# First loads of a fused sequence-mixing and gated-MLP kernel: x's first block in two halves, weights ahead of x's last blocks, another order of turns and quarters

## The chip, the cores and the metric

The kernel runs on one core of a Trainium2 chip. The metric is the device time of one execution in microseconds (us). A core has five engines that run side by side and wait for each other by semaphores: PE (TensorE, matrix products), DVE (VectorE), ACT (ScalarE), POOL (GpSimd) and SP (SyncE, which here only issues DMA transfers). Weight loads of PE are listed apart as PEld. ACT issues a few DMA transfers too. All transfers, whichever engine issues them, run on the core's 16 DMA engines.

## The reference

```python
x  = A_q                                  # 2048 x 640, bfloat16
xn = _layernorm(x, axis=-1)               # mean and variance of each row
return x + _A_ref(xn, A_k, A_v, A_shift_k, A_ssm_k, A_ssm_D) + _B_ref(xn, B_w_gate, B_w_up, B_w_down)

def _A_ref(q, k, v, shift_k, ssm_k, ssm_D):
    # k is filtered with four taps along the sequence, kv = k_shift * v,
    # y = kv convolved along the sequence with ssm_k (by FFT of twice the length) + kv * ssm_D
    return q * y

def _B_ref(x, w_gate, w_up, w_down):      # 640 x 1728, 640 x 1728, 1728 x 640
    g = jnp.einsum("bsd,df->bsf", x, w_gate)
    u = jnp.einsum("bsd,df->bsf", x, w_up)
    h = _sigmoid(g) * u
    return jnp.einsum("bsf,fd->bsd", h, w_down)
```

## The kernel before

The 2048 rows are 16 blocks of 128 rows, taken in four groups of four. x is a tile of 128 partitions by 16 blocks by 640 columns of two bytes, so one block is 160 KB. For each group the kernel normalises four blocks (`ln_stats` L198, `ln_aggr` L202, `ln_var` L210 on DVE, `ln_pow` L214 on POOL, `ln_xn` L219 on DVE). It then turns each block: `xn_mm` (L234) makes five 128x128 transposes on PE into a PSUM tile `pt`, and `xn_ev` (L223) copies them on ACT to `xnT`. After that come the gated products: for each of 13 chunks `fc` of 128 columns, and one last half chunk, PE makes `pg` (w_gate) and `pu` (w_up) from five matmuls each over all 512 rows of the group (`product`, L257), ACT takes the sigmoid of `pg` (L266) and DVE multiplies it with `pu` into `hT` (L272). `down_mm` (L296) multiplies `hT` with w_down, and DVE adds the result to x (L301). The convolution (lines 309 to 466) has products of its own on PE, copies on ACT, multiplications on DVE and round trips of its intermediate results through HBM.

The program runs in the order in which it is written. After the prologue this order is the long string `ORDER` (L621), of which each letter is one step of one chain; each engine takes its own instructions strictly in that order, and the change does not touch the string.

The prologue, which the change does touch, is this:

- Loads. SP issues x's block 0 (L469), then 256 columns of w_gate, 320 KB (L173 by L473), then the next 256 columns of both weights (L475). ACT issues block 1 (L470), blocks 2 and 3 in one transfer of 320 KB (L471), and the first 256 columns of w_up, 320 KB (L176 by L473). Between its first and its second DMA, ACT has a table load and a warming activation (L119). A transfer of SP and one of ACT go through different queues, called q1 and q10 by the profile. The program has eight semaphores for its DMA transfers and uses them in turn, so a transfer can be issued only when the one eight before it has landed. The first that has to wait is SP's load of columns 512 to 768 of w_up, the second step of `ORDER`.
- `busy(15)` (L482): 15 matmuls of 128x512 on zeros, whose result is not used.
- Statistics and normalising of blocks 0 to 3, in this order on DVE: statistics of block 0; statistics of block 1, then xn of block 0; statistics of block 2, then xn of block 1; and so on. So xn of a block stands behind the statistics of the next block.
- `turn(0)`, that is `xn_mm` and `xn_ev` of block 0, and `busy(2)`.
- For the first two chunks of the first group the products are made in quarters (`quarter`, L248), five 128x128 matmuls for one block, one chunk and one of the two weights, so that PE can start with block 0 while the others are still on their way. There are 16 quarters. The turns of blocks 1 to 3 stand between them: turn 1 after two quarters of block 0, turn 2 after two quarters of block 1, and turn 3 after all four of block 1.
- Two sigmoids and two multiplications on the finished chunks; then the first dense product (L257) of `ORDER` begins.

PE takes its instructions in order: when a quarter waits for weights, the turn behind it waits too.

Of the kernel before, what the change touches and what calls it, by code (L numbers as in the profile page):

```python
# [57 lines left out]
def kernel(  # L58
# [14 lines left out]
    nc = tc.nc  # L73
    xr = A_q.flatten_outer_dims().rearrange("(p b) d -> p b d", b=NB)
# [30 lines left out]
    x = res.tile([P, NB, DM], BF16, name="x")  # L105
# [15 lines left out]
    sync = nc.sync  # L121
# [49 lines left out]
    def load_w(eng, lo, hi, u):  # L171
        if u == 0:
            eng.dma_start(w[:, :, lo:hi], wgr[:, :, lo:hi])  # L173
            return
        h = min(hi, 13 * P)
        eng.dma_start(w[:, :, UP + lo:UP + h], wur[:, :, lo:h])  # L176
        if hi == FF:
            eng.dma_start(w[:, :, FF:UP], wur[:, :, h:FF])
# [51 lines left out]
    def xn_mm(g, i):  # L230
        pool, tag = (psG, "g") if g else (psC, "c")
        xts[i] = pt = pool.tile([P, NC, P], BF16, name="pt", tag=tag)
        for c in range(NC):
            nc.tensor.transpose(pt[:, c, :], xn[:, 4 * g + i, c * P:(c + 1) * P], ident[:])  # L234

    def xn_ev(g, i, copy=act_copy):
        copy(out=xnT[:, i, :, :], in_=xts[i][:, :, :])
# [4 lines left out]
    def quarter(u, fc, i):  # L242

        if i == 0:
            pgs[u, fc] = psG.tile([P, 512], F32, name=("pg", "pu")[u], tag="g")
        o = u * UP + fc * P
        for c in range(NC):
            nc.tensor.matmul(pgs[u, fc][:, i * P:(i + 1) * P], lhsT=w[:, c, o:o + P], rhs=xnT[:, i, c, :],  # L248
                             start=(c == 0), stop=(c == NC - 1))
# [216 lines left out]
        nc.vector.tensor_tensor(xs, xs, chunks[c]["yx", m][:, :, :], ALU.add)  # L466


    sync.dma_start(x[:, 0, :], xr[:, 0, :])  # L469
    nc.scalar.dma_start(x[:, 1, :], xr[:, 1, :])  # L470
    nc.scalar.dma_start(x[:, 2:4, :], xr[:, 2:4, :])  # L471
    for u in range(2):
        load_w((sync, nc.scalar)[u], 0, 256, u)  # L473
    for u in range(2):
        load_w(sync, 256, 512, u)  # L475

# [3 lines left out]
    def busy(n):  # L480
        for _ in range(n):
            nc.tensor.matmul(idle[:, :], lhsT=hT[:, 0, 0:P], rhs=hT[:, 0, :], start=True, stop=True)  # L482

    def turn(i):
        xn_mm(0, i)
        xn_ev(0, i)


    busy(15)
    for i in range(4):  # L490
        ln_stats(0, i)
        if i:
# [5 lines left out]
    turn(0)  # L498
    busy(2)
    for i in range(4):  # L500
        for fc in range(2):
            for u in range(2):
                quarter(u, fc, i)
            if (i, fc) in ((0, 0), (1, 0), (1, 1)):
                turn(1 + i + fc)
    for fc in range(2):
        gate_ev(0, fc)
        up_ev(0, fc)
# [158 lines left out]
```

## Time and profile before

| what | value |
|---|---|
| median of 3 runs | 239.65 us (239.36 to 239.73) |
| the profiled execution | 239.41 us |
| its span, first to last instruction | 237.6 us |
| granted clock of PE | 1.00 in every stretch |
| PE, DVE, ACT busy | 231.4, 190.3, 141.2 us |
| first DMA packets, first statistics on DVE | after 1.5 us, at 3.97 us |
| first turn, first quarter, first dense product on PE | at 6.54, 7.78 and 14.34 us |

The span is the time between the first and the last instruction of the profiled execution; the rest of that execution's time lies around it. In the list of waits each row names who waited, for whom, the total in us, how often, and the longest. In the rows in order of time, the first number is the start from the beginning of the span, the second the duration, then engine, line, operation, result and operands, shape, how many instructions were merged, and in brackets the idle time before them with what ended it. Matmuls overlap in the pipeline, so of successive groups on PE the starts tell more than the durations. A row of the table by stretch gives the busy time of each engine in it, PE's granted clock, the share of time in which the DMA engines were busy, and the GB/s that they moved; these rates are added up to the bytes moved by a time:

| stretch, us | GB/s |
|---|---|
| 1.5 to 2.5 | 73 |
| 2.5 to 3.0 | 317 |
| 3.0 to 3.5 | 341 |
| 3.5 to 4.0 | 394 |
| 4.0 to 5.0 | 372 |
| 5.0 to 6.0 | 303 |
| 6.0 to 7.0 | 293 |
| 7.0 to 8.0 | 294 |

### The profile page before, as it was taken

The numbers are of one execution on the slowest core, as the hardware profiler recorded it, in microseconds if no ns is written. First come the engines' busy times: TensorE is split into PE (matmuls) and PEld (weight loads), VectorE is DVE, ScalarE is ACT, GpSimd is POOL, SyncE is SP. The second block draws the span as 40 slices with busy tenths as digits, with TensorE's granted clock in tenths as the row PEclk, the third lists the DMA queues.
The fourth block names the chain that finished last, engine by engine and source line by source line (L and its number), as shares of the span: only waits on it lengthen the run. The fifth ranks groups of instructions, "written<-read, shape, count | busy, mean of one in ns | idle before, by whom it ended". The sixth has DMA issues, their size and how long they took to land.

```text
span 237.6 us, 5553 instructions
## 1 busy us (share of the span) xinstructions
PE 231.4 (97%) x2265; PEld 135.1 (57%) x2265; DVE 190.3 (80%) x350; ACT 141.2 (59%) x178; POOL 11.2 (5%) x24
## 2 busy tenths in 40 slices
PE   8799999999999999999999999999999999999994
PEld 2564445878556455667754434577664434456782
DVE  3633889999999999999999999865585695968372
ACT  2342331728559897864888887997558858764000
POOL 4210000020000000002001000000000000000000
PEclk9999999999999999999999999999999999999999
DMA  7999999889998999999444888975939795285674
GB/s 212 292 314 233 259 322 298 183 249 284 253 311 243 253 295 297 284 267 319 148 183 152 234 230 258 227 228 203 241 109 222 186 281 123 89 238 144 196 237 134
DMA packets 88975, 54.82 MB, mean 231 GB/s; under 512 B 47670, under 2 KB 83062, under 8 KB 88694
## 3 DMA queue, kind: packets, MB, share of 16 engines
q1 hardware_dynamic: 88006, 53.66, 80.8%
q10 hardware_dynamic: 944, 0.82, 1.1%
q8 instruction: 17, 0.28, 0.5%
q14 instruction: 8, 0.07, 0.1%
HBM read 36.12 MB, written 18.35 MB: 229 GB/s over the span
## 4 chain that ended last, share of the span: by engine, by line
PE 95%; DMA 3%; ACT 0%; DVE 0%; ACTq 0%; issue 0%
PE pd L296 26%; PE pg L257 23%; PE pu L257 23%; PE psb L456 4%; PE ps L357 4%; PE ps L355 4%; PE ps L388 3%; DMA w<-in_B_w_up_dram 3%; PE psa L417 2%; PE pg L278 2%; PE pt L234 2%; PE pu L248 1%; PE pg L248 1%; ACT xnT L223 0%; DVE x L301 0%; ACT L119 0%
## 5 line engine op out<-in xcount | busy, mean ns | idle before, releaser
L257 PEld LDWEIGHTS <-w 128*128 128x128 bf16 x500 | 46.5, 98 | 54.3 <-issue 5.3
L296 PE MATMUL pd<-wd,hT 128*128 128x320 bf16 x448 | 64.3, 299 | 0.0
L257 PE MATMUL pg<-xnT,w 128*128 128x512 bf16 x250 | 62.2, 379 | 0.0
L257 PE MATMUL pu<-xnT,w 128*128 128x512 bf16 x250 | 62.1, 379 | 0.0
L296 PEld LDWEIGHTS <-hT 128*128 128x128 bf16 x448 | 42.8, 98 | 17.8 <-issue 1.7
L266 ACT ACTIVATE sig<-pg 128x512 bf16<-128x512 f32 x52 | 31.3, 605 | 30.1 <-PE pg L257 28.2
L272 DVE TENSOR_TENSOR hT<-sig,pu 128x512 bf16<-128x512 bf16 x52 | 35.2, 679 | 14.7 <-PE pu L257 9.3
L223 ACT CAST t<-ps 128x1024 bf16<-128x1024 f32 x40 | 39.1, 1023 | 11.4 <-DMA d<-t 6.3
L223 ACT CAST xz<-ps 128x1024 bf16<-128x1024 f32 x40 | 38.6, 1018 | 10.6 <-PE ps L388 10.5
L301 DVE TENSOR_TENSOR x<-pd,x 128x320 bf16<-128x320 f32 x32 | 15.4, 480 | 15.8 <-PE pd L296 15.7
L403 DVE TENSOR_TENSOR xz<-xz 128x2048 bf16<-128x2048 bf16 x20 | 24.4, 1220 | 0.2
L357 PE MATMUL ps<-kvh,S1t 128*128 128x128 bf16 x160 | 21.2, 219 | 0.0
L335 DVE TENSOR_TENSOR acc<-acc,tmp 128x1024 bf16<-128x1024 bf16 x30 | 20.7, 689 | 0.7
L355 PE MATMUL ps<-kvh,S1t 128*128 128x128 bf16 x160 | 21.2, 217 | 0.0
L333 DVE TENSOR_TENSOR tmp<-kx,sc 128x1024 bf16<-128x1024 bf16 x30 | 20.6, 687 | 0.4
L223 ACT CAST ao<-psa 128x1024 bf16<-128x1024 f32 x16 | 15.6, 1014 | 5.6 <-PE psa L417 3.5
L461 DVE TENSOR_TENSOR yx<-psb,xn 128x512 bf16<-128x512 f32 x20 | 13.8, 691 | 3.9 <-PE psb L456 2.9
L355 PEld LDWEIGHTS <-S1t 128*128 128x128 bf16 x160 | 15.5, 97 | 2.3
L357 PEld LDWEIGHTS <-S1t 128*128 128x128 bf16 x160 | 15.3, 96 | 2.3
L223 ACT COPY xnT<-pt 128x640 bf16<-128x640 bf16 x16 | 10.2, 709 | 10.8 <-PE pt L234 10.5
L198 DVE BATCH_NORM_STATS2 st<-x 128x6 f32<-128x320 bf16 x32 | 13.7, 471 | 2.8 <-DMA x<-in_A_q_dram 2.8
L401 DVE STREAM_SHUFFLE xz<-xz 128x512 f32<-128x512 f32 x20 | 14.6, 728 | 0.0
(44 smaller groups left out, 146.1 us busy)
## 6 DMA issues: line engine op xcount, KB each, us to landing
d<-t SPq DMA_DIRECT2D x20, 512.0 KB, 3.7
t<-d SPq DMA_DIRECT2D x20, 512.0 KB, 4.9
bi<-d SPq DMA_DIRECT2D x8, 512.0 KB, 5.5
d<-ao SPq DMA_DIRECT2D x6, 512.0 KB, 4.1
kx<-in_A_k_dram SPq DMA_DIRECT2D x10, 256.0 KB, 5.0
hn<-in_A_ssm_k_dram SPq DMA_DIRECT2D x20, 128.0 KB, 6.0
kvh<-in_A_v_dram SPq DMA_DIRECT2D x10, 256.0 KB, 5.2
x<-in_A_q_dram SPq DMA_DIRECT2D x3, 640.0 KB
```

The source lines that it names most:

```text
L223: nc.scalar.copy(out=out, in_=in_)
L257: nc.tensor.matmul(pg[:, :], lhsT=w[:, c, u * UP + fc * P:u * UP + (fc + 1) * P], rhs=xnT[:, :, c, :], start=(c == 0), stop=(c == NC - 1))
L266: nc.scalar.activation(sig[fc][:, :], pgs[0, fc][:, :], ACT.Sigmoid)
L272: nc.vector.tensor_tensor(hT[:, fc, :], sig[fc][:, :], pgs[1, fc][:, :], ALU.mult)
L296: nc.tensor.matmul(pd[:, :], lhsT=hT[:, fc, bb * P:(bb + 1) * P], rhs=wd[:, fc, 320 * half:320 * half + 320], start=(fc == 0), stop=(fc == ...
L301: nc.vector.tensor_tensor(x[:, 4 * t + bb, es], pds[bb, half][:, :], x[:, 4 * t + bb, es], ALU.add)
L333: nc.vector.tensor_tensor(d["tmp"][:, :, :], kx[:, lo + 3 - m:hi + 3 - m, :], sb(m), ALU.mult)
L335: nc.vector.tensor_tensor(d["acc"][:, :, :], d["acc"][:, :, :], d["tmp"][:, :, :], ALU.add)
L355: nc.tensor.matmul(ps[:, i, 0:P], lhsT=S1[:, b, h, :], rhs=cin[c]["kvh"][:, 0, b, :], start=True, stop=True)
L357: nc.tensor.matmul(ps[:, i, P:2 * P], lhsT=S1[:, b, h, :], rhs=hp[:, b // 2, b % 2, :], start=True, stop=True)
L401: nc.vector.stream_shuffle(z[:, 2, :, :].bitcast(F32), z[:, 1, :, :].bitcast(F32), swap)
L403: nc.vector.tensor_tensor(z[:, 1:3, :, :], z[:, 0:1, :, :].to_broadcast((P, 2, 8, P)), z[:, 1:3, :, :], ALU.mult)
```

## The change

Block 0 of x is loaded in two halves of 320 columns, one by SP and one by ACT. Then SP loads the first 256 columns of w_gate, block 2, and the next 256 columns of both weights; ACT loads block 1, the first 256 columns of w_up, and block 3. The warming matmuls before the first turn are 11 instead of 15. Turns 1, 2 and 3 each stand directly behind the first quarter of the block before. For block 0 the order of quarters is now w_gate of both chunks and then w_up of both; for the other blocks it stays. With two transfers more in the prologue, the turn of the eight semaphores makes ACT's load of block 3 wait for the landing of the first block's half on ACT's queue, and SP's loads from the third block of weight columns on wait for others of the first transfers than before. The instructions of DVE and POOL and all of `ORDER` are the same.

```diff
-    sync.dma_start(x[:, 0, :], xr[:, 0, :])
+    for i in range(2):
+        (sync, nc.scalar)[i].dma_start(x[:, 0, 320 * i:320 * i + 320], xr[:, 0, 320 * i:320 * i + 320])
+    load_w(sync, 0, 256, 0)
     nc.scalar.dma_start(x[:, 1, :], xr[:, 1, :])
-    nc.scalar.dma_start(x[:, 2:4, :], xr[:, 2:4, :])
-    for u in range(2):
-        load_w((sync, nc.scalar)[u], 0, 256, u)
+    load_w(nc.scalar, 0, 256, 1)
+    sync.dma_start(x[:, 2, :], xr[:, 2, :])
+    nc.scalar.dma_start(x[:, 3, :], xr[:, 3, :])
     for u in range(2):
         load_w(sync, 256, 512, u)
...
-    busy(15)
+    busy(11)
...
     for i in range(4):
-        for fc in range(2):
-            for u in range(2):
-                quarter(u, fc, i)
-            if (i, fc) in ((0, 0), (1, 0), (1, 1)):
-                turn(1 + i + fc)
+        for k in range(4):
+            fc, u = divmod(k, 2) if i else (k % 2, k // 2)
+            quarter(u, fc, i)
+            if k == 0 and i < 3:
+                turn(i + 1)
```

## The prediction

> **What bounds the kernel now.** I read the page first, then who waited for whom, then the rows in order of time of the first 15 us, and last the table by stretch.
>
> ```profile
> PE 231.4 (97%) x2265; PEld 135.1 (57%) x2265; DVE 190.3 (80%) x350; ACT 141.2 (59%) x178; POOL 11.2 (5%) x24
> PE   8799999999999999999999999999999999999994
> DVE  3633889999999999999999999865585695968372
> DMA  7999999889998999999444888975939795285674
> ```
>
> TensorE is busy 97% of 237.6 us; only its first and last slices are low. In the list of waits from 11 us to the end no row of PE stands at all. So a time saved before PE becomes dense is saved at the end, if nothing that PE needs later stays where it is. Waits from 0 to 11 us:
>
> ```profile
> DVE st L198 <- DMA x<-in_A_q_dram: 2.8, 1, 2.8
> ...
> PE pu L248 <- DMA w<-in_B_w_up_dram: 0.6, 1, 0.6
> PE pt L234 <- DVE xn L219: 0.6, 1, 0.6
> PE pg L248 <- ACT xnT L223: 0.6, 2, 0.3
> ```
>
> PE loses 1.7 us in four gaps: to the first normalised block, to its copy out of PSUM, to w_up's columns, to a later copy. The rows (start, duration, engine and line):
>
> ```profile
> 3.97 0.89 DVE L198 BATCH_NORM_STATS2 st<-x 128x6 f32<-128x320 bf16 x2 [2.85 <-DMA x<-in_A_q_dram]
> ...
> 6.54 0.45 PE L234 MATMUL pt<-ident,xn 128*128 128x128 bf16 x5 [0.57 <-DVE xn L219]
> ...
> 6.71 0.88 DVE L198 BATCH_NORM_STATS2 st<-x 128x6 f32<-128x320 bf16 x2
> ...
> 7.50 0.43 DVE L219 TENSOR_SCALAR xn<-x,mv,rstd 128x640 bf16<-128x640 bf16 x1
> ...
> 7.78 0.44 PE L248 MATMUL pg<-xnT,w 128*128 128x128 bf16 x5 [0.35 <-ACT xnT L223]
> ...
> 8.81 0.45 PE L248 MATMUL pu<-xnT,w 128*128 128x128 bf16 x5 [0.60 <-DMA w<-in_B_w_up_dram]
> ...
> 9.10 0.44 PE L234 MATMUL pt<-ident,xn 128*128 128x128 bf16 x5
> ...
> 9.58 0.69 ACT L223 COPY xnT<-pt 128x640 bf16<-128x640 bf16 x1 [1.85 <-PE pt L234]
> ...
> 10.32 0.44 PE L248 MATMUL pg<-xnT,w 128*128 128x128 bf16 x5 [0.22 <-ACT xnT L223]
> ...
> 14.34 0.59 PE L257 MATMUL pg<-xnT,w 128*128 128x512 bf16 x2
> ```
>
> At 8.81 the third gap ends: w_up's first 256 columns, issued at 1.65, landed 7.12 us later (the chain of waits begins with it). Behind it stood the turn of block 1, whose xn had been ready since 7.93. From 10.32 PE runs without a gap into the dense products at 14.34. This 14.34 is what the change can move.
>
> **The change, part by part.** One turn or one quarter occupies PE 0.28 us (10.60, 10.88, 11.16, 11.44 are successive starts). A turn's start to its ACT copy is 0.48 (9.10 to 9.58), the copy 0.69, and PE starts 0.05 after it (10.27 to 10.32).
>
> *x's first block in halves.* Before, block 0 on SP's queue and block 1 on ACT's (160 KB each) shared the DMA engines; block 0 landed 3.2 us after 0.73, at 3.95. Now only 160 KB are under way at first. At the 317 to 341 GB/s of 2.5 to 3.5 us, 160 KB less are worth 0.47 us; at worst nothing, since each queue still has 128 rows. I take 0.4, near the upper row because the engines were full from 2.5 us on. Block 0's chain on DVE and POOL follows: xn(0) ends at 6.1 instead of 6.49, its quarter starts at 7.38 instead of 7.78. w_gate's columns were in by 7.05 (PE loaded weights then) and are not later now: less of x is ahead of them.
>
> *Block 1* is now issued on ACT behind the first half, the table load and the warming activation, at about 1.22, where blocks 2 and 3 were issued; it is needed at 4.8 (5.21 less 0.4). Some 470 KB (both blocks and a part of w_gate) are out near 3.7 by the rates; with the 0.7 to 0.9 of the next paragraph it lands at 4.4 to 4.6. If it were 0.3 late, block 2's wait would hide it.
>
> *Block 2* is the price. It was in the second transfer of ACT's queue and in by 5.6 (1.22 plus 4.4). Now it is the third on SP's, behind 320 KB of w_gate. Ahead of its last byte go x0 and x1 (320 KB), w_gate (320), itself (160) and most of w_up's 320 on the other queue, which takes turns: from 6 to 7 us the two queues sent 308 and 278 packets. That is about 1060 KB. The first 160 KB are out at 2.8; 900 KB at 293 GB/s (6 to 7 us, all 512-byte rows) take 3.1, at 341 take 2.6: last byte at 5.4 to 5.9. Landing follows the last byte by 0.7 (x0: 320 KB were out at 3.26 by the rates, landed 3.95) to 0.9 (w_up: last packets near 7.9, landed 8.77), and up to 1.5 where both queues were full (w_gate's second 256 columns). So it lands between 6.1 and 7.5; I take 6.9, the 293 GB/s row with some of the crowding. DVE wants it at 6.31 and waits 0.6. Queued behind that wait is xn(1), then all later statistics.
>
> *Turns one product sooner.* Turn 1 now follows the first quarter, and three quarters stand behind it. It starts 1.29 after block 2's landing: 0.02 to the statistics, 1.22 from their start to xn(1)'s end (6.71 to 7.93), 0.05 to PE: 8.19, against 9.10. From here the order sets the pace: turn to copy 0.48, copy 0.69, 0.05, one quarter 0.28, next turn: 1.50 a block. The three quarters between (0.84) fit beside copy and wait. Turns at 8.19, 9.69, 11.19; last block's quarters at 11.19 + 1.22 = 12.41; four quarters, 1.12; dense products at 13.53. xn(2) and xn(3) end at 9.59 and 11.01, in time. The rule is: dense start = turn 1 + 5.34. That is 0.81 earlier than 14.34.
>
> *w_up* is now needed at 8.75 and has one block of x less ahead on its queue (160 KB against 480); its bytes end about with block 2's, so it lands near 7.1. Even at its old 8.77 it would cost nothing measurable.
>
> *Block 3* waits on ACT for the first half's landing before it is issued (eight DMA semaphores go round; SP's later loads wait likewise, with over 1 MB queued in front, so no DMA engine runs dry). It is wanted at 8.4. Its 160 KB and as much of w_gate follow block 2, 1.0 us more, so it lands near 7.9; 0.3 late would cost 0.3 or less, PE having 0.1 to 0.2 of slack at turn 2.
>
> *Four warming matmuls fewer* free 0.85 us of PE in which it would idle anyway. The weight loads at 1.58, 2.01 ... 3.72 are 0.43 apart, from 4.08 on 0.2: the array had become fast after 2.9 us of work. Eleven still cover this, but PE then idles 1.1 us before turn 0, where the longest gap of the fast time is 0.60. The Trainium skill, "TensorE: Matmul & The Clock Gate", Part 1 (The HAM clock gate), says that the clock falls only after an idle window of about 3.4 us, which would leave the sum alone; it also says that the window runs free and that one kernel saw 6, 11 or 14 slow matmuls. By the last, eleven might not be enough, which is the third rival below; the granted clock of this trace is 1.00 in every stretch and does not tell.
>
> *After 13.5.* Does the 0.8 survive? DVE is full from 32 to 140 us (9.77 of 10 us in 40:50, 39.15 of 40 in 60:100), but its last idle time, at 31.87, ended with a PE product, so it moves with PE. DMA is full until 40 us and does not move. By the trace's semaphore events the transfers it must deliver came 1.4 us early (k, wanted at 23.85), 1.1 early (the second filter chunk, 43.98) and 1.5 early (x's second group, 46.00). All exceed 0.8. I keep all of it; the lower bound is none of it.
>
> Sum: the profiled execution took 239.41 for a span of 237.6; less 0.81 that is 238.6. The median shown is 239.65, 0.24 above that execution, so for a median I say 238.85.
>
> **Rivals.**
> 1. *Block 2 in time.* If it lands by 6.3, turn 1 follows the first quarter at 7.66 and the dense products start at 13.0: 1.34 gained, 238.3 (238.2 with x0's 0.47). For it: two queues at 341 to 400 GB/s until 5 us. Against it: most bytes are now weights in 512-byte rows, at 293.
> 2. *The gain is lost later.* A transfer fixed by the full DMA queue, or ACT's copies (in 50:60 ACT waited for DMA writes, 4.4 us), stops PE: 239.2 to 239.8. For it: DVE and DMA are as full as PE. Against it: the margins of 1.1 us and more.
> 3. *The array runs slow after the shorter warming*: slower. Place: turn 0 and the quarters. It decides if the array needs more than 11 x 0.43 = 4.7 us of work; the trace had 2.9. Price: another 2.9 us of work at half speed, 1.45 lost on a chain of PE groups, against 0.81: 240.3.
> 4. *Block 2 very late.* At 7.7 the sum is nil, at 8.0 it is 0.3 slower, 239.95; w_gate's second columns, 7.92 before, are the nearest row.
>
> **How the numbers follow.** Measurement can tell about 0.2%, 0.48 us, from no change. Forecast (block 2 at 6.6 to 7.3, gain 0.4 to 1.1): 0.45, of which 0.05 falls within 0.2%. Rival 1: 0.22, faster. Rival 2, with block 2 at 7.3 to 7.8: 0.19, same. Rivals 3 and 4 beyond 7.8: 0.08 and 0.06, slower. So faster 0.62, same 0.24, slower 0.14. The range takes in the forecast and rivals 1 and 2 and stops at rival 4's beginning, short of rival 3: 238.1 to 239.9.
>
> **What would show it.** Right: DVE's first statistics near 3.6; its third pair waits for x until about 6.9; turn 1 near 8.2; no PE wait for w_up; dense products near 13.5; no PE wait behind. Wrong: third statistics at 6.3 without a wait (rival 1); quarters 0.56 instead of 0.28 apart (rival 3); new PE waits after 20 us (rival 2).

## The result, and the profile after

The changed kernel takes 240.99 us (median of 22 runs, 239.99 to 241.86); the kernel before took 239.62 beside it (22 runs, 239.29 to 240.58). The ratio is 1.005, 95% interval 1.0039 to 1.0061: **slower by half a per cent**. The forecast was 238.85, faster, in a range that ended at 239.9. Its profiled execution took 240.04 with a span of 238.2, 0.6 us more than before.

The page of the changed kernel, the rows that answer to those of before:

```profile
PE 232.2 (97%) x2261; PEld 135.1 (57%) x2261; DVE 190.8 (80%) x350; ACT 141.0 (59%) x178; POOL 11.1 (5%) x24
...
PE   8899999999999999999999999999999999999994
...
DVE  4634889999999999999999999865585695968372
...
DMA  6999999989996999979344888975949695285674
```

TensorE looks as full as before. What moved is 0.9 us, too little for slices of 6 us. The rows in order of time show the prologue (start, duration, engine and line):

```profile
1.18 4.88 PE L484 MATMUL idle<-hT 128*128 128x512 bf16 x11 [1.18 <-DVE hT L117]
...
2.99 0.89 DVE L198 BATCH_NORM_STATS2 st<-x 128x6 f32<-128x320 bf16 x2 [1.86 <-DMA x<-in_A_q_dram]
...
5.01 0.89 DVE L198 BATCH_NORM_STATS2 st<-x 128x6 f32<-128x320 bf16 x2 [0.70 <-DMA x<-in_A_q_dram]
...
6.30 0.67 PE L234 MATMUL pt<-ident,xn 128*128 128x128 bf16 x5 [0.24 <-DVE xn L219]
6.46 0.88 DVE L198 BATCH_NORM_STATS2 st<-x 128x6 f32<-128x320 bf16 x2
...
7.75 0.44 PE L248 MATMUL pg<-xnT,w 128*128 128x128 bf16 x5 [0.35 <-ACT xnT L223]
...
8.03 0.44 PE L234 MATMUL pt<-ident,xn 128*128 128x128 bf16 x5
...
8.76 0.89 DVE L198 BATCH_NORM_STATS2 st<-x 128x6 f32<-128x320 bf16 x2 [0.77 <-DMA x<-in_A_q_dram]
...
10.05 0.45 PE L234 MATMUL pt<-ident,xn 128*128 128x128 bf16 x5 [0.36 <-DVE xn L219]
...
11.56 0.44 PE L234 MATMUL pt<-ident,xn 128*128 128x128 bf16 x5
...
13.91 1.24 PE L257 MATMUL pg<-xnT,w 128*128 128x512 bf16 x5
```

Statistics of block 0 start 0.98 earlier than before (3.97). Turn 1 is at 8.03, 1.07 earlier than before. But DVE's fourth statistics wait 0.77 for block 3 (8.76), so turn 2 comes 2.02 after turn 1, not 1.50. The dense products start at 13.91 instead of 14.34: **0.43 gained**.

How much is gained differs from execution to execution, and block 3 decides it. Eight of the executions in this document, this one and seven below, have these loads and this order. Block 3 landed in them between 8.74 and 9.30, and each time the dense products started 5.17 after that landing: at 13.91 to 14.47, which is 0.43 earlier to 0.13 later than before.

This gain does not last. In what follows, "offset" is the start of a PE instruction minus the start of the same one in the kernel before. It is -0.43 at 14 us and -0.50 at 120 us; from 126 us to the end it is +0.45. All of the loss, 0.95, falls at one place. The list of waits from 11 us to the end, which had no row of PE before, has one now:

```profile
PE psa L417 <- ACT t L223: 0.5, 1, 0.5
```

The rows around it, first in the kernel before, then in the changed one (an SPq row is a transfer's issue; its x3 counts the issues merged in it):

```profile
118.50 5.68 SPq L369 DMA_DIRECT2D d<-t  x3
118.85 2.19 ACT L223 CAST t<-ps 128x1024 bf16<-128x1024 f32 x2
121.91 1.93 ACT L223 CAST t<-ps 128x1024 bf16<-128x1024 f32 x2 [0.21 <-DMA d<-t]
...
124.06 0.65 PE L417 MATMUL psa<-xz,SMt 32*32 32x512 bf16 x32
```

```profile
118.00 6.81 SPq L369 DMA_DIRECT2D d<-t  x3
118.35 2.19 ACT L223 CAST t<-ps 128x1024 bf16<-128x1024 f32 x2
122.53 1.93 ACT L223 CAST t<-ps 128x1024 bf16<-128x1024 f32 x2 [1.34 <-DMA d<-t]
...
123.60 0.39 PE L417 MATMUL psa<-xz,SMt 32*32 32x512 bf16 x2
124.51 0.65 PE L417 MATMUL psa<-xz,SMt 32*32 32x512 bf16 x30 [0.53 <-ACT t L223]
```

ACT casts products from PSUM to a tile `t`, SP writes `t` to HBM (L369, 512 KB), and the next casts may overwrite that buffer only when the write has landed. The write is issued 0.50 earlier in the changed kernel, as everything is, but lands at 122.44 instead of 121.81: 4.44 us after its issue instead of 3.31. So ACT's next casts start 0.62 later than before, and PE waits.

Why did the same write take 1.13 longer? The page has a DMA queue that neither the kernel nor I had spoken of:

```profile
q8 instruction: 17, 0.28, 0.5%
```

17 packets of 16 KB: 0.28 MB over PE's 4522 instructions (2261 matmuls and as many weight loads) is 62 bytes each, one packet per 266; from the first of these packets (14.63 us) to the last (220.42 us) PE started 253 instructions per packet. I read them as the fetches of PE's own program. The Trainium skill ("Runtime: NRT & Kernel Launch", Instruction fetch mechanics) says that instructions are fetched in blocks of 16 KiB, 256 instructions, by a DMA queue of the engine's own, and that the cost is mostly hidden; the size and the count agree with this trace. Each such packet takes 0.88 to 1.56 us in the changed kernel, where a 4 KB packet of the write takes 0.16. A write has 128 such packets and 16 closing ones of 4 bytes, one for each DMA engine. In the kernel before a fetch started at 118.78, ahead of the write's first packet at 119.32; fifteen engines closed their part of the write by 120.75, the sixteenth at 121.33. In the changed kernel it started at 120.16, when three data packets of the write were still to come on that engine. The other fifteen closed by 120.24; the sixteenth went on at 121.07, by then in company with the next write, and closed at 121.94. In both kernels the write landed 0.5 after its last closing packet. No other traffic is in the way: from 117.8 to 124.5 us both traces have the packets of two such writes and the one fetch, and nothing else.

Four warming matmuls fewer are eight instructions fewer (each has a weight load). If the fetches come at fixed counts of instructions, every later fetch stands eight instructions further on in the program. That was the theory to be tested. Around 118 us eight instructions are four products of 512 columns, 0.86 us; the fetch came 1.89 later against the write's issue (2.16 instead of 0.27), so the count alone does not give the whole shift.

### The profile page after: what moved, and what is told of

The parts are those of the page before. It is cut to its first block, busy times and chain, and to the rows that moved or that the text cites. A ratio compares the mean times of both kernels' runs of the same rounds, so it can differ in the third digit from the quotient of the medians.

```text
span 238.2 us, 5547 instructions
## 1 busy us (share of the span) xinstructions
PE 232.2 (97%) x2261; PEld 135.1 (57%) x2261; DVE 190.8 (80%) x350; ACT 141.0 (59%) x178; POOL 11.1 (5%) x24
## 4 chain that ended last, share of the span: by engine, by line
PE 89%; DMA 5%; ACT 2%; issue 1%; DVE 1%; ACTq 0%
PE pd L296 25%; PE pu L257 22%; PE pg L257 22%; PE psb L456 4%; DMA x<-in_A_q_dram 3%; PE ps L357 3%; PE ps L355 3%; PE ps L388 3%; PE psa L417 2%; DMA d<-t 2%; PE pg L278 2%; PE pt L234 2%; ACT t L223 1%; ACT xz L223 1%; PE pu L248 1%
```

## The experiments

Theories: **A**, eight PE instructions fewer move the fetch behind the start of the write at 118, which costs about 1 us at 124. **B**, the shorter warming leaves the array slow for longer. **C**, any earlier start is taken back at a transfer that doesn't move with it. Edits are against the changed kernel where nothing else is said. The ratios are against the kernel before in runs on the same chip, with its median 239.40 for the first four kernels, 239.76 for narrow13 to x3_ahead15, 239.45 for order15 to tiny4 and 239.61 for x3_sp15.

**after_again**: the changed kernel once more, without an edit.

> The changed kernel once more, for a second trace. In the first trace its dense products began 0.43 us earlier than before (13.91 against 14.34) and it lost 0.87 us at 124 us, where a 16 KB instruction fetch ran beside a write of d1. Theory A (instruction fetches: eight PE instructions fewer shift the fetches against the program, and one now meets that write): dense products near 13.9 again, a PE wait of about 0.5 to 0.9 at 124 us or at another such write, 240.0 to 241.0. Theory B (slow array: eleven warming matmuls end before the array has become fast, at a moment that differs from run to run): dense products anywhere from 13.6 to 15.5, and the time varies by more than 1 us between runs. Theory C (any earlier start of PE meets the late writes): as A.

240.33 us, 1.0038 (1.0026 to 1.0049). Dense products at 14.14, offset -0.28 at 120 us and +0.77 behind 124: loss 1.05 at the same place, the only PE wait after 11 us the same row. The fetch started 1.04 after the write's issue and took 1.49.

**warm15**: all of the change except the shorter warming.

```diff
-    busy(11)
+    busy(15)
```

> The changed kernel with 15 warming matmuls again, loads and order as changed. Theory A: the PE instruction count is as before, so are the places of the fetches; the 0.4 us won early are kept: 239.0 to 239.4. Theory B: the array is fast in time in every run: 239.0 to 239.3 and no spread over 0.6 us. Theory C: the count of warming matmuls does not matter, 240.5 to 241.

239.32 us, 0.9991 (0.9979 to 1.0002). No PE wait behind 11 us. The fetch is back at 0.54 after the issue, the write lands 3.57 after it, and the offset is +0.01 at the end. The 0.4 that A wanted kept was not won in this execution: block 3 landed at 9.17 and the dense products started at 14.34.

**narrow15**: 15 warming matmuls of 376 columns, which is the work of 11 wide ones. It keeps the count of before and the short warming.

```diff
-            nc.tensor.matmul(idle[:, :], lhsT=hT[:, 0, 0:P], rhs=hT[:, 0, :], start=True, stop=True)
+            nc.tensor.matmul(idle[:, 0:cols], lhsT=hT[:, 0, 0:P], rhs=hT[:, 0, 0:cols], start=True, stop=True)
...
-    busy(11)
+    busy(15, 376)
```

> The changed kernel with 15 warming matmuls of 376 columns instead of 11 of 512: the same warming time, the instruction count of before. Theory A: 239.0 to 239.4. Theory B: as the changed kernel, 240.5 to 241 with a spread over 1 us. Theory C: 240.5 to 241. So A and B part here.

239.25 us, 0.9997 (0.9981 to 1.0012). No loss at 124; offset -0.29 at the dense products and -0.33 at the end. With warming as short as in the changed kernel, B would have kept the loss.

**before_warm11**: the kernel before, with the shorter warming alone.

```diff
-    busy(15)
+    busy(11)
```

> The kernel before with 11 warming matmuls, loads and order as before. Theory A: the fetches shift as in the changed kernel without the early gain: 240.3 to 241.3. Theory B: PE turns slow in part of the runs: 240 to 241.5 with a spread over 1 us; dense products later than 14.34 in the trace. Theory C: 239.6, since PE does not start earlier.

240.40 us, 1.0046 (1.0022 to 1.007). Here w_up landed late in the profiled execution (PE waited 1.25 for it, dense products 0.85 later than before), so nothing started early. Yet the same loss stands at 124: +0.78 to +1.91. C falls as the cause of this loss: it needs an early start.

**narrow13** and **narrow19**: the same work in other counts.

```diff
-    busy(11)
+    busy(13, 434)
```

```diff
-    busy(11)
+    busy(19, 297)
```

> The changed kernel with 13 warming matmuls of 434 columns: the warming time of 11 x 512, four PE instructions more than it and four fewer than 15. Theory A (the place of the instruction fetch decides): the fetch near 119 us stands halfway between those of 15 and 11; the loss at 124 us is between none and 0.9, so 239.2 to 240.3, and the trace shows the fetch and the write overlapping by as much. Rival C2 (it is the length of the warming that costs, not the count): as the other kernels with this length, which gave 240.33 with 11 and 239.25 with 15, so no common value.

> The changed kernel with 19 warming matmuls of 297 columns: the same warming time, eight PE instructions more than with 15. Theory A: the fetch near 119 us comes earlier against the program than with 15, before the write's packets: no loss at 124 us, 239.0 to 239.5, unless another fetch now meets a write that PE soon needs. Rival: if any count other than 15 is bad (the order string fits 15 only), 240.0 or more.

239.49 us, 0.9995 (0.9973 to 1.0016), and 240.18, 1.0035 (1.0015 to 1.0056). Neither loses anything at 124 (fetch 0.16 and 0.28 behind the issue). Both lose at a place where the changed kernel does not: 0.60 and 0.53 at 77 us, narrow19 another 0.24 at 55. A alone does not tell of this; it comes back below. Nor did the fetch stand where A had said: halfway for 13 and earlier for 19. In both it was where 15 have it.

**late8**: the changed kernel, 11 warming matmuls, with the eight instructions put back at 110 us. In the first block of the third group, column block 0 is transposed five times instead of once.

```diff
-        for c in range(NC):
+        for c in range(NC) if (g, i) != (2, 0) else (0, 0, 0, 0, 0, 1, 2, 3, 4):
```

> The changed kernel with its 11 warming matmuls, and eight more PE instructions just before the third group's turns (the first transpose of that group is made four times more, about 0.2 us of PE at 110 us). Theory A: from there on the fetches stand in the program where they stood with 15, the wait at 124 us is gone: 239.3 to 239.7. Theory B (a slow array in the prologue) or any cause in the first 20 us: the loss stays, 240.4 to 240.7.

239.94 us, 1.0013 (0.9986 to 1.0039). This is the clearest test of the count, by its trace: the prologue is that of the changed kernel, only the count ahead of the write is mended, 100 us later. Its time tells less: 239.94 lies between A's 239.3 to 239.7 and B's 240.4 to 240.7, and the interval overlaps that of after_again. The rows of this kernel at the write:

```profile
118.76 5.91 SPq L369 DMA_DIRECT2D d<-t  x3
119.11 2.19 ACT L223 CAST t<-ps 128x1024 bf16<-128x1024 f32 x2
122.40 1.93 ACT L223 CAST t<-ps 128x1024 bf16<-128x1024 f32 x2 [0.44 <-DMA d<-t]
...
124.32 0.70 PE L417 MATMUL psa<-xz,SMt 32*32 32x512 bf16 x32
```

The casts wait 0.44 instead of 1.34, PE not at all; the write lands 3.54 after its issue. The offset is +0.25 ahead of 124 (the four extra transposes) and +0.31 behind: the loss has gone from 0.95 to 0.06.

**x3_ahead15**: block 3 ahead of w_up on ACT's queue, 15 warming matmuls.

```diff
     nc.scalar.dma_start(x[:, 1, :], xr[:, 1, :])
+    nc.scalar.dma_start(x[:, 3, :], xr[:, 3, :])
     load_w(nc.scalar, 0, 256, 1)
     sync.dma_start(x[:, 2, :], xr[:, 2, :])
-    nc.scalar.dma_start(x[:, 3, :], xr[:, 3, :])
```

> The changed kernel with 15 warming matmuls, and block 3 of x ahead of w_up's first columns on ACT's queue. Theory P (the last block's landing, 8.7 to 9.2 in the traces, holds DVE's last statistics and so the dense start): block 3 lands near 6.5, w_up near 7.7 and in time; dense products at 12.8 to 13.4, 238.1 to 238.7. Rival Q (the turn order or block 1, which landed at 5.0, sets it): dense start stays at 13.9 to 14.3, 239.2. Rival R (a gain of over 0.4 us is lost to transfers that do not move): dense start early, new PE waits between 20 and 60 us, 238.9 to 239.2.

240.61 us, 1.005 (1.0023 to 1.0076), which no theory had. Block 3 landed at 6.22, but w_up, now last on that queue, at 10.38; PE waited 1.7 for it and the dense products came 0.78 late. Whatever is fourth on ACT's queue is late. It is also issued late, at 3.23 here (block 3 at 3.14 in the changed kernel), because it waits for the first half's landing; no run parts this from its place behind three others.

**order15**: the loads of before, the changed order of turns and quarters, 15 warming matmuls.

```diff
-    for i in range(2):
-        (sync, nc.scalar)[i].dma_start(x[:, 0, 320 * i:320 * i + 320], xr[:, 0, 320 * i:320 * i + 320])
-    load_w(sync, 0, 256, 0)
+    sync.dma_start(x[:, 0, :], xr[:, 0, :])
     nc.scalar.dma_start(x[:, 1, :], xr[:, 1, :])
-    load_w(nc.scalar, 0, 256, 1)
-    sync.dma_start(x[:, 2, :], xr[:, 2, :])
-    nc.scalar.dma_start(x[:, 3, :], xr[:, 3, :])
+    nc.scalar.dma_start(x[:, 2:4, :], xr[:, 2:4, :])
+    for u in range(2):
+        load_w((sync, nc.scalar)[u], 0, 256, u)
```

> The loads of the kernel before, the changed order of turns and quarters, 15 warming matmuls. Theory A (the loads cost, not the order; and with the old count of instructions the fetch of PE's instructions stands ahead of the write at 118): turn 1 directly behind the first quarter, 8.06; w_up at 8.8 holds block 0's third quarter for 0.2; turns 2 and 3 near 9.65 and 11.15, dense products at 13.4 to 13.6 (0.8 sooner than before), write of 118 landing within 3.6 of its issue, no wait of PE at 124: ratio 0.9955 to 0.998, 238.5 to 239.0. Rival (whatever the prologue gains is taken back where the DMA queue is full, at 72 to 77 or at 124): dense at 13.5, a new wait of PE behind 50, ratio 0.998 to 1.001.

239.18 us, 0.9986 (0.9959 to 1.0014). The dense products start at 13.64, 0.70 earlier: in this execution the new order alone gains more there than all of the change did in any. Of this 0.37 is lost at 77 and 0.32 at 124, and the end stands where it stood (offset -0.01). The waits of PE from 11 us on:

```profile
PE ps L355 <- ACT t L223: 0.2, 1, 0.2
```

So the time and the losses behind 50 came as the rival had said. The fetch was in its old place here (0.27 behind the issue) but took 1.40 instead of 0.92, and the write landed at 121.98, hardly other than the 121.81 of before.

**loads15**: the other way about, the loads of the change with the order and the 15 warming matmuls of before.

```diff
-            fc, u = divmod(k, 2) if i else (k % 2, k // 2)
-            quarter(u, fc, i)
-            if k == 0 and i < 3:
-                turn(i + 1)
+                quarter(u, fc, i)
+            if (i, fc) in ((0, 0), (1, 0), (1, 1)):
+                turn(1 + i + fc)
```

> The changed loads, the order of turns and quarters of the kernel before, 15 warming matmuls. Theory A: block 3 of x lands at 8.7 to 9.2 and sets the third turn at 11.4 or later, so the new order is worth nothing beside these loads: dense at 13.9 to 14.4, ratio 0.998 to 1.000. If the order were what gains and the loads were harmless: dense at 13.5 needs the new order, and this kernel would stay at 14.3 with block 3 landed before 8.4.

239.5 us, 0.9984 (0.9961 to 1.0007). Dense products at 13.97, and the 0.37 stays to the end (-0.44). Block 3 landed at 8.67, and turn 3 came at 11.40, as in the changed kernel (11.56): beside these loads the order is worth little.

**halves_order15**: the loads of before with only block 0 in halves; the changed order, 15 warming matmuls.

```diff
-    load_w(sync, 0, 256, 0)
     nc.scalar.dma_start(x[:, 1, :], xr[:, 1, :])
-    load_w(nc.scalar, 0, 256, 1)
-    sync.dma_start(x[:, 2, :], xr[:, 2, :])
-    nc.scalar.dma_start(x[:, 3, :], xr[:, 3, :])
+    nc.scalar.dma_start(x[:, 2:4, :], xr[:, 2:4, :])
+    for u in range(2):
+        load_w((sync, nc.scalar)[u], 0, 256, u)
```

> Only block 0 in two halves, the other loads as before; the changed order; 15 warming matmuls. Theory A: statistics of block 0 at 3.0 to 3.2, block 1 about 4.9, blocks 2 and 3 together near 6.2, w_up near 8.8 as before, which then sets the pace: dense at 13.2 to 13.6, no wait of PE behind: ratio 0.995 to 0.998. Rival (gains are taken back where the DMA queue is full): ratio 0.998 to 1.001 with a new wait of PE behind 50.

240.67 us, 1.0044 (1.0021 to 1.0066), which neither theory had. w_up, now the fourth transfer on ACT's queue, landed at 10.10. The table by stretch of this kernel (stretch, its length, busy time and count of PE, PEld, DVE, ACT and POOL, granted clock, DMA share, GB/s):

```profile
8.00:10.50 2.50, 1.08 (x17) 0.91 (x18) 1.77 (x8) 0.69 (x1) 1.10 (x2) 1.00 1.17 290
10.50:12.00 1.50, 1.50 (x19) 1.50 (x17) 0.30 (x1) 0.00 (x0) 0.00 (x0) 0.55 1.16 292
12.00:14.00 2.00, 2.00 (x22) 2.00 (x20) 0.00 (x0) 0.69 (x1) 0.63 (x1) 0.50 1.18 290
14.00:16.00 2.00, 2.00 (x36) 1.93 (x35) 0.00 (x0) 0.97 (x2) 0.00 (x0) 0.98 1.16 294
```

PE was busy 1.08 of 2.5 us, its longest gap 1.42, and then the granted clock was 0.50 until 14 us: groups 0.53 apart instead of 0.28, dense products 2.03 late. The third rival of the prediction had named a slow array too, but from a shorter warming; here 15 warming matmuls had run, and w_up's lateness thinned the work. The Trainium skill ("TensorE: Matmul & The Clock Gate", Part 1) has the clock fall after an idle window of about 3.4 us; here there was no such idle stretch, only sparse work: PE was busy 1.68 of the 3.41 us from 7.24 to the fall at 10.65.

**tiny4**: four warming matmuls of 64 columns behind the eleven wide ones.

```diff
     busy(11)
+    busy(4, 64)
```

> The changed kernel with four more warming matmuls of 64 columns, so eight more instructions of PE in 0.2 us at most. Theory A: dense as in the changed kernel, 13.9 to 14.3; the fetch starts within 0.6 of the issue of the write at 118 and the write lands within 3.6 of it; no loss at 124: ratio 0.998 to 1.000, 239.0 to 239.5. If it were the shorter warming itself that costs: loss at 124 stays, 240.2 to 240.9.

239.44 us, 0.9996 (0.9977 to 1.0015), clear of the 1.0026 to 1.0049 of after_again. Fetch 0.25 behind the issue, nothing lost at 124: four matmuls of next to no work do what four wide ones do. (Dense products at 14.47, block 3 having landed at 9.30.)

**x3_sp15**: block 3 on SP's queue behind block 2, 15 warming matmuls. What was open: is block 3 late by its place or by bytes alone, and is a gain near 0.8 kept once the fetch is in place?

```diff
-    sync.dma_start(x[:, 2, :], xr[:, 2, :])
-    nc.scalar.dma_start(x[:, 3, :], xr[:, 3, :])
+    for i in (2, 3):
+        sync.dma_start(x[:, i, :], xr[:, i, :])
```

> The changed kernel with block 3 on SP's queue directly behind block 2 (ahead of columns 256 to 512), and 15 warming matmuls. Theory P (in the changed kernel block 3, last on ACT's queue, is late because half of the bytes until 8.7 go to SP's later weight columns): block 3 lands at 6.5 to 7.5, w_up at 7.0 to 8.3, no statistics wait behind block 2's, turn 1 near 8.0, turns 1.5 apart, dense products at 13.3 to 13.6. If instead bytes alone limit it, block 3 or w_up comes at 8.7 again and dense is at 13.9 or later. What is kept of it: if only the place of PE's fetch decides (15 warming matmuls put it back), 238.5 to 238.9, ratio 0.996 to 0.998, no wait of PE behind 13; if gains beyond 0.4 are taken back at 72 to 77 and 124 by the full DMA queue, as one execution of the kernel with the old loads and the new order showed, 239.0 to 239.5, ratio 0.998 to 1.000, with new waits of ps at 77 or psa at 124.

239.39 us, 0.9992 (0.997 to 1.0013). Block 3 landed at 7.20 and w_up at 6.71; the rows:

```profile
7.68 0.88 DVE L198 BATCH_NORM_STATS2 st<-x 128x6 f32<-128x320 bf16 x2
...
8.46 0.44 PE L234 MATMUL pt<-ident,xn 128*128 128x128 bf16 x5
...
9.96 0.44 PE L234 MATMUL pt<-ident,xn 128*128 128x128 bf16 x5
...
11.46 0.44 PE L234 MATMUL pt<-ident,xn 128*128 128x128 bf16 x5
...
13.80 1.24 PE L257 MATMUL pg<-xnT,w 128*128 128x512 bf16 x5
```

No statistics wait after block 1's, and the turns are 1.50 apart: it was the place, with the earlier issue (2.20 instead of 3.14), and not the bytes. (Turn 0 stood behind the warming until 6.96, so 13.80 and not the 13.5 expected.) The fetch is in place and nothing is lost at 77 or 124, but of the 0.54 gained 0.44 is lost between 53 and 56 us, where the list of waits from 45 to 56 us has ACT once more behind a write (4.4 in the kernel before). The time is that of the theory that gains are taken back, at another place than the two that it had named. I take this wait of ACT for the cause; no run tried it:

```profile
ACT t L223 <- DMA d<-t: 5.3, 1, 5.3
```

All executions side by side; the losses are read from PE's offset, and everything is in us:

| kernel | fetch start after the write's issue at 118 | issue to landing | offset at dense | lost at 53-56 | at 77 | at 124 |
|---|---|---|---|---|---|---|
| before | 0.27 | 3.31 | 0 | 0 | 0 | 0 |
| the changed kernel | 2.16 | 4.44 | -0.43 | 0 | 0 | 0.95 |
| after_again | 1.04 | 4.54 | -0.21 | 0 | 0 | 1.05 |
| before_warm11 | 1.18 | 4.62 | +0.85 | 0 | 0 | 1.13 |
| warm15 | 0.54 | 3.57 | 0.00 | 0 | 0 | 0.08 |
| narrow15 | 0.12 | 3.40 | -0.29 | 0 | 0 | 0 |
| narrow13 | 0.16 | 3.31 | -0.13 | 0 | 0.60 | 0 |
| narrow19 | 0.28 | 3.45 | -0.31 | 0.24 | 0.53 | 0 |
| late8 | 0.17 | 3.54 | -0.02 | 0 | 0 | 0.06 |
| x3_ahead15 | 0.34 | 3.41 | +0.78 | 0 | 0.22 | 0 |
| order15 | 0.27 | 3.81 | -0.70 | 0.07 | 0.37 | 0.32 |
| loads15 | 0.37 | 3.36 | -0.37 | 0 | 0 | 0 |
| halves_order15 | 0.14 | 3.38 | +2.03 | 0 | 0 | 0 |
| tiny4 | 0.25 | 3.49 | +0.13 | 0 | 0.17 | 0 |
| x3_sp15 | 0.18 | 3.44 | -0.54 | 0.44 | 0 | 0 |

The three kernels whose fetch starts 1 us or more after the issue lose 0.95 to 1.13 at 124; the twelve others at most 0.32.

But the fetches do not simply move with the count. Counted in the program, the fetch near 118 starts at the same instruction, to within 2, in those twelve, whether they have 13, 15 or 19 warming matmuls; in after_again, before_warm11 and the changed kernel it starts 10, 16 and 28 instructions later, where A had 8. And from 185 us on, the fetches of these three stand within 6 instructions of those of the kernel before. So it is shown that eight instructions fewer put this one fetch late; what sets the place of a fetch is not.

No version beats the kernel before by more than its interval.

What stays open is the loss at 77. The five kernels that lose there are those whose first read of a round trip (L379, issued near 62) took 6.6 to 7.2 us instead of 5.5 to 6.4. No fetch stands out in its place there, and what slowed that read was not found. The profiled executions also explain less than the medians: the changed kernel's span is 0.6 longer, its median time 1.37 in one set of runs and 0.93 in the other.

## Why the prediction was wrong, point by point

- *Block 0 in halves*, 0.4 earlier: right in kind, mis-sized; the second half was in 0.83 earlier (3.12). Yet the first quarter was at 7.75, not 7.38, because of the next point.
- *Block 1 at 4.4 to 4.6, no wait*: 4.98, and DVE waited 0.70. Between the first halves and what followed them the DMA engines moved only 78 to 146 GB/s (2.75 to 3.25 us); I had counted 317 to 341 there. The statistics of block 1 stand ahead of xn(0), so turn 0 came at 6.30; without that wait it would still have stood behind the warming until 6.06.
- *Block 2 is the price, 6.9*: it landed at 5.97 and nobody waited. That is rival 1's condition, but its 13.0 did not follow, for block 3 was late.
- *w_up near 7.1*: 6.96, right. *Turn 1 at 8.19*: 8.03, near by luck: it followed from block 1's lateness, not from block 2's.
- *Block 3 near 7.9, harmless*: this step failed in the prologue. It landed at 8.74 (8.67 to 9.30 in the eight other kernels with these loads), and with it fell "dense start = turn 1 + 5.34": 13.37 by the rule, 13.91 in fact. Counted from block 3 the prediction's own terms fit: 1.29 to turn 2, 1.50 to turn 3, then 1.22 and 1.12, together 5.13, and 5.17 was found. I had put block 3 one microsecond behind block 2; but it is the fourth transfer on ACT's queue, and by its turn SP's queue was sending columns 256 to 512, which nobody needs before the dense products. x3_sp15 showed that its place is the cause, with the earlier issue that goes with a place on SP's queue (2.20 instead of 3.14), and not the bytes as such.
- *Four warming matmuls fewer are free*: this step failed for the whole. I priced their time, 0.85 of idle PE, and never asked what their count moves. It put the fetch at 118 late, which costs 0.95 to 1.13: late8 and tiny4 gave the count back and took the loss away, and before_warm11 made the loss by the count alone. The time was mis-sized too. Eleven did not cover the slow phase in this execution: their weight loads stayed 0.43 apart to the last, they ended at 6.06 where fifteen had ended at 5.97, and PE idled 0.24 before turn 0, not 1.1. So rival 3's condition came true (4.88 us of work, and still slow), but cost only about 0.2 (0.67 for the five transposes of turn 0 against 0.45), not 1.45.
- *After 13.5 I keep all of it*: this step failed as well. I looked at three transfers up to 46 us, which had 1.1 to 1.5 of margin, and not at the writes that free ACT's `t` buffers later on, though rival 2 named the 4.4 us of such waits. At 121.91 ACT waited 0.21 for such a write in the kernel before; that is a place where a gain of the start can be lost again. order15 and x3_sp15, whose fetch was in place, lost all of 0.70 and 0.44 of 0.54 at 53 to 56, 77 and 124; loads15 and narrow15 kept 0.37 and 0.29.
- The rivals: the second had the kind, a wait of ACT for a write, but the place that it named (50 to 60) is where x3_sp15 lost and not the changed kernel, and its price stopped at the gain (239.2 to 239.8). It lacked a cause that takes more than what was won.

By steps, in the profiled execution: 0.81 forecast, 0.43 found at the dense products (block 3), 0.07 more by 120 us, then 0.95 lost at 124.

## What to carry to other kernels

When instructions are added to or taken from a long unrolled program, even idle ones, count them, and look where that engine's instruction fetches stand afterwards: here eight fewer in the first 6 us put a fetch at 118 us onto a transfer with no margin, which cost about 1 us. Before a gain at the start is carried to the end, look at every wait that ends with a DMA all the way down, also on engines that are not the bottleneck; a transfer that just comes in time is a wait in the making. If the change's own count of instructions can be put right with a few tiny ones, measure that too before judging the rest.

## What the runs showed of the hardware that was not expected

- A fetch of PE's instructions (16 KB, one per about 253 instructions) took 0.88 to 1.56 us in the changed kernel, and the part of a write on one of the 16 DMA engines waited behind it. Starting 1.0 to 2.2 us after the issue of a 512 KB write, it made that write land 4.4 to 4.6 us after its issue; starting within 0.6 us, 3.3 to 3.8. What the Trainium skill ("Runtime: NRT & Kernel Launch", Instruction fetch mechanics) calls mostly hidden is hidden from PE itself, which had no wait for a fetch in the lists, but not from a transfer behind the fetch.
- The granted clock fell to 0.50 after a wait of 1.42 us in sparse work, and came back about 3.4 us later.
- In x3_ahead15 a PE wait of 1.7 us near the same place left the granted clock at 1.00. From w_up's first quarter to the dense products it took 4.69 us, and 6.22 in halves_order15 with the same order: the same kind of gap costs about 1.5 us more, or nothing. What decides is open.
- The warming products become fast at moments that differ between executions: their weight loads, first 0.43 apart, are 0.2 apart from 4.08 us on in the kernel before and from 5.72 on in order15, both with 15 of them.
